# The 64-row parts of two products' low weights, in pairs of matmuls on the upper and lower rows of the array

## The chip, the cores and the metric

The kernel runs on one core of a Trainium2 chip. The metric is the device time of one execution in microseconds (us); the median of three runs of the kernel before is 1816.04 us (1814.41 to 1816.51). A core has five engines with a queue of instructions each: TensorE (PE in the profile; its weight loads are listed as PEld), VectorE (DVE), ScalarE (ACT), GpSimd (POOL) and SyncE (SP), which here only issues transfers. An engine works its queue in order. Engines wait for each other through semaphores.

## The reference

The input `x` has 8192 rows of 448 numbers. It is normalised row by row, and the result `xn` goes two ways:

```
xn = layernorm(x)                                   # 8192 x 448
s  = irfft( softshrink( mlp2( relu( mlp1( rfft(xn) )))))   # along the 8192 rows; 4 blocks of 112 channels
g  = silu( (gelu(xn @ w_gate) * (xn @ w_up)) @ w_down )    # 448 -> 1792 -> 448
out = x + s * g
```

`s` is the spectral part, `g` the feed-forward part, and the change lies in the feed-forward part's first two products, `xn @ w_up` and `xn @ w_gate`, which have a contraction of 448 = 3 x 128 + 64.

## The kernel before

Float32 numbers are held as two float16 numbers, high and low, and a product of two such numbers is three matmuls: high by high, high by low, low by high. The feed-forward products go by a scheme of seven products on halves of the operands (numbered 1 to 7 in the code, in the order 1, 5, 6, 2, 3, 7, 4), where sums and differences of the operands are made ahead. The rows of `x` are taken in 16 chunks of 512 rows, a chunk as two half chunks of 256, and the 1792 hidden columns in 14 tiles of 128. There are two passes over the chunks: the first with 8 of the tiles, whose weights stay in fast memory, the second with the other 6 (`PF`, line 30). The first two chunks of the first pass are done in a plain way. In all others the tiles are taken two at a time; such a pair is a *unit* (line 1026): four units for a chunk of the first pass, three for one of the second, 14 x 4 + 16 x 3 = 104 in all.

In a unit the seven products add up in three banks of the accumulator memory: X (ring `bx`, two banks), Y and Z (ring `by`, two banks). `a1` to `a7` are the steps that issue one product each, for both tiles of the unit:
- `a1` puts product 1 into X, ScalarE copies it out (`p1`); `a5` puts product 5 into Y, ScalarE copies it (`p5`); `a6` adds product 6 into X, ScalarE copies it (`v1`).
- `a2` puts product 2 into Z, and then VectorE adds Z to `p1` (`c11`, rows `u<-by,u` in the profile), ScalarE applies gelu to the sum.
- `a3` adds product 3 into Y, and VectorE adds Y to `v1` (`c12`, rows `v<-by,v`), then multiplies it with the gelu (rows `wt<-v,fc,u` in the second pass), which gives half of `h`.
- `a7` adds product 7 into X, and VectorE adds X and `p5` into `v2` (`c22`, rows `v<-bx,u`).
- `a4` adds product 4 into X. It waits until `c22` has read X. Then ScalarE applies gelu straight from X and VectorE multiplies it with `v2` (`c21`).

Products 1, 5, 6 and 7 are of two blocks of 128 rows: six matmuls for a tile, 12 for a unit. Products 2, 3 and 4 are of 192 rows, that is of one block of 128 rows and one of 64. The block of 128 takes three matmuls. In the block of 64 rows (`v + 1` and `xb + 1` in `product`, line 985) the high weights stand twice, in the upper and in the lower 64 rows, and the operand from `x` has its high part in one half of the rows and its low part in the other; so one matmul of 128 rows gives high by high and high by low. The fifth matmul of the five is low weights by the same operand. So products 2, 3 and 4 take 5 matmuls for a tile, 10 for a unit, each of 256 columns.

The order of a unit's steps is the list at the end of `unit` (line 1154); `a4` of a unit is issued ahead of the third step of the next one (`chunk`, line 1442). The last unit of a chunk has no next one. In the first pass, the down projection of the earlier tiles then stands between (`down`, line 1365). In the second pass `down2` (line 1251) begins with that `a4`; here, and only here, the list of before has `a7` ahead of `a3`.

All instructions are issued by a planner (`Pace`, line 49): tasks are generators, each with a due time; an instruction gets a cost by `Pace.cost` (line 168), and a task goes on when the planner's clock says that its input is there. It fixes the order in every engine's queue at build time, nothing more; on the chip the engines only follow it. `B` (class `Either`, line 204) gives an operation to VectorE or to GpSimd, whichever ends first by these costs. Beside the first pass the planner runs the first stage of the transform and the making of operands (`factors`, line 532, writes the sums of halves of `xn` that the products use to a scratch tensor, from which they are read transposed); beside the second pass the spectral stage (`group`, line 1702) and, after it, the last transform (`tiles3`, line 1814). Their matmuls stand between those of the units; they use the ring `bf`.

Every instruction is recorded by one helper, so all rows have line 199, and groups are told apart by the names of their tiles: `wt` are weights (of which two serve as buffers in the second pass), `xta` and `xtb` the transposed operands (`xtb` that of products 2, 3 and 4), `h` the hidden values, `dw` the weights down, `u,mt` the last transform.

Of the kernel before, what the change touches and what calls it, by code (L numbers as in the profile page):

```python
# [10 lines left out]
F16 = mybir.dt.float16  # L11
# [18 lines left out]
PF = ((0, 8), (8, 6))  # L30
PB = ((0, 5), (5, 8))
K1, K2 = 256, 192
# [16 lines left out]
class Pace:  # L49
# [118 lines left out]
    def cost(self, e, op, start, out, ins):  # L168

        n, sb, psum = self.wide(out, ins)  # L170
        extra = sum(n > 1 and i.free_size() == 1 for i in ins)
        if e == "PE":
            n = out.free_size()
            return max(0.049, n * 0.000423 + 0.001) * (4 if ins[0].dtype == F32 and op == "matmul" else 1)
        if e == "ACT":
            return (0.14 if psum else 0.18) + 0.00086 * n + 0.1 * extra
        if e == "POOL":
            t = 1.1 if n < 8 and op == "tensor_tensor_pow" else 0.2 + 0.0023 * n
        elif n < 32:
            return 0.17  # L180
        elif psum or sb < 2 and op != "tensor_scalar":
            return 0.14 + 0.00107 * (n + 60 * (extra > 0))
        else:
            t = (0.12 + 0.00112 * n if sb >= 2 else 0.15 + 0.0008 * n) + 0.06 * (extra > 0)
        other, ahead = ("POOL", 0.15) if e == "DVE" else ("DVE", 0.0)
        return t + max([b - start - ahead for a, b in self.port[other] if a <= start < b] + [0.0])
# [187 lines left out]
def afno_geglu_kernel(ctx, tc, x, gu, wd, mlp, b1, b2, c_m, c_mt, c_small, out):  # L374
    nc = tc.nc
    pace = Pace()
    V, S, G, T, Q = (Engine(pace, n, e) for n, e in (
        ("DVE", nc.vector), ("ACT", nc.scalar), ("POOL", nc.gpsimd), ("PE", nc.tensor), ("SP", nc.sync)))
    B = Either(pace, V, G, 0.0)
# [50 lines left out]
    wt = [cp.tile([128, 2, 16, 128], F16, name=f"wt{f}") for f in range(PF[0][1])]  # L430
# [26 lines left out]
    EV = {}  # L457

    def ev(*key):
        return EV.setdefault(key, Event())  # L460
# [71 lines left out]
    def factors(c, q, xs):  # L532

        xn = EV["x4", c][:, 2 * q:2 * q + 2, :]
        sf = yield from SF.get()
        sx = yield from SX.get()
        S.copy(sf[:, 0, K2:], xn[:, 1, K2:K1])
        B.tensor_add(sf[:, 0, 0:K2], xn[:, 1, 0:K2], xn[:, 1, K1:])
        B.tensor_sub(sf[:, 2, :], xn[:, 0, 0:K1], xn[:, 1, 0:K1])
        yield  # L540
        B.tensor_sub(sf[:, 1, :], sf[:, 0, :], xn[:, 0, 0:K1])
        yield
        B.tensor_sub(sf[:, 3, 0:K2], xn[:, 0, K1:], sf[:, 1, 0:K2])
        big = sx[:, 0:6 * K1].rearrange("p (k s c) -> p k s c", k=3, s=2)
        low = sx[:, 6 * K1:]
        S.copy(big[:, :, 0, :], sf[:, 0:3, :])
        yield
        S.copy(low[:, 0:K2], sf[:, 3, 0:K2])
        B.tensor_sub(big[:, :, 1, :], sf[:, 0:3, :], big[:, :, 0, :])
        yield  # L550
        B.tensor_sub(low[:, K2:K1], sf[:, 3, 128:K2], low[:, 128:K2])
        B.tensor_sub(low[:, K1:], sf[:, 3, 0:128], low[:, 0:128])
        SF.put(sf)
        yield
        rows = xts[c % NG][128 * q:128 * q + 128]
        Q.dma_start(rows[:, 2 * K1:2 * K1 + 4 * 480], sx)
        SX.put(sx)
        yield ev("lo", c, q)
        Q.dma_start(rows[:, 0:2 * K1].rearrange("p (s c) -> p s c", s=2), xs[:, 0, :, 0:K1])
        low = rows[:, 2 * K1 + 4 * 480:].rearrange("p (k c) -> p k c", k=2)  # L560
        Q.dma_start(low[:, :, 0:K2], xs[:, :, 0, K1:])
        Q.dma_start(low[:, :, K2:K1], xs[:, :, 1, D - 64:])
        Q.dma_start(low[:, :, K1:], xs[:, :, 1, K1:K1 + 128])
        yield
# [410 lines left out]
    PROD = {1: (0, 4), 5: (4, 8), 6: (8, 10), 7: (12, 12), 2: (3, 6), 4: (6, 14), 3: (0, 2)}  # L975
# [6 lines left out]
        yield  # L982
        done("xt", kind, first, i)

    def product(k, bank_, xT, f0, first, last):
        xb, v = PROD[k]
        for e in range(2):
            w = wt[f0 + e]
            if k in (1, 5, 6, 7):
                seq = [(s, v + j, xb + 2 * d + j) for j in range(2) for s, d in ((0, 0), (0, 1), (1, 0))]  # L990
            else:
                seq = [(0, v, xb), (0, v, xb + 2), (1, v, xb), (0, v + 1, xb + 1), (1, v + 1, xb + 1)]
            for n, (s, vv, xx) in enumerate(seq):
                T.matmul(bank_[:, 256 * e:256 * e + 256], w[:, s, vv, :], xT[:, xx, :],
                         start=first and e == 0 and n == 0, stop=last and e == 1 and n == len(seq) - 1,
                         skip_group_check=True)


    state = {"direct": NG}

# [5 lines left out]
    def gelu(p, f0, gl, src):  # L1006
        for cs, b in scaled(p, f0):
            S.activation(gl[:, cs], src[:, cs], AF.Gelu_apprx_tanh, scale=fc[:, 4, b:b + 1])
# [17 lines left out]
    def unit(p, i, f0, h, xa):  # L1026

        m = {}
# [9 lines left out]
        def a1():  # L1038
            for e in range(2):
                yield ev("comb", f0 + e) if p == 0 else ev("far", f0 + e)  # L1040
            m["X"] = yield from BX.get()
            product(1, m["X"], xa, f0, True, False)
            copy_of(U1, "p1", m["X"], pace.last)

        def a5():
            m["Y"] = yield from BY.get()
            product(5, m["Y"], xa, f0, True, False)
            copy_of(U5, "p5", m["Y"], pace.last)

        def a6():  # L1050
            yield m["ep1"]
            product(6, m["X"], xa, f0, False, False)
            copy_of(V1, "v1", m["X"], pace.last)

        def a2():
            m["Z"] = yield from BY.get()
            product(2, m["Z"], EV["xtb", p, i], f0, True, True)
            m["c11"] = pace.spawn(c11(), pace.last)

        def c11():  # L1060
            u = m["p1"]
            V.tensor_tensor(u, m["Z"], u, op=ALU.add)
            BY.put(m["Z"])
            yield
            gelu(p, f0, u, u)
            yield

        def a3():
            yield m["ep5"]
            product(3, m["Y"], EV["xtb", p, i], f0, False, True)  # L1070
            pace.spawn(c12(), pace.last)

        def c12():
            yield m["ev1"]
            v = m["v1"]
            V.tensor_tensor(v, m["Y"], v, op=ALU.add)
            BY.put(m["Y"])
            yield
            yield m["c11"]
            if p == 1:  # L1080
                g0 = m["g0"] = yield from G0.get()

                def back():
                    V1.put(v)
                    U1.put(m["p1"])

                yield from glu(p, f0, m["p1"], v, 0, h, back, g0)
                done("h", p, i, f0, 0)
                return
            yield from glu(p, f0, m["p1"], v, 0, h, lambda: V1.put(v))  # L1090
            U1.put(m["p1"])
            done("h", p, i, f0, 0)
# [33 lines left out]
        def sums(gl):  # L1126
# [24 lines left out]
            G0.put(g0)  # L1151
            pace.then(lambda: done("hs", i, f0, 0))

        return [a1, a5, a6, a2, a7, a3] if p == 1 and f0 == PF[1][1] - 2 else [a1, a5, a6, a2, a3, a7], a4

    def plain(c, f):

# [284 lines left out]
    def chunk(p, i):  # L1442
# [19 lines left out]
        for u in range(nf // 2):  # L1462
            six, last = unit(p, i, 2 * u, h, xa)
            for n, s in enumerate(six):
                if (u, n) == (0, 2) and "tail" in state:
                    yield from state.pop("tail")()
                if (u, n) == (0, 3):
                    yield ev("xt", "b", p, i)
                if n == 2 and prev:
                    yield from prev()  # L1470
                    if (p, i) == (0, NG - 1):
                        pace.spawn(far_pair(u - 1))
                    yield pe()
                yield from s()
                yield pe()
            prev = last
# [639 lines left out]
```

## Time and profile before

| | us |
|---|---|
| median of three runs | 1816.04 |
| span of the profiled execution, first to last instruction | 1811.1 |
| TensorE busy | 1769.5 (98%) |
| VectorE busy | 1395.7 (77%) |
| ScalarE busy | 1059.9 (59%) |
| GpSimd busy | 470.3 (26%) |
| granted TensorE clock, mean | 0.998 |

The page gives the span of the profiled execution and no other time of its own; the median of the runs is 4.9 us longer.

A row of a group reads: line, engine, operation, tile written <- tiles read, shapes, count, then after the bar the busy time in us, the mean time of one in ns, and the idle time of the engine just before them with what ended it. A matmul's shape 128*128 is rows and columns of the array, and then what streams through. A row of the timeline reads: start in us, length in us, engine, line, operation, shape and count; in brackets stands idle time before it and what ended it. Matmuls are pipelined: the length of a row holds the time until its last result is out, so a matmul's slot is read from the distance of two starts.

### The profile page before, as it was taken

What the parts mean: (1) busy time and instruction counts of PE and PEld (TensorE: products, weight loads), DVE (VectorE), ACT (ScalarE), POOL (GpSimd) and SP (SyncE); (2) the same over time, 40 slices, a digit from 0 to 9 for tenths busy, and PEclk for the clock granted to TensorE, in tenths of its full rate; (3) what the DMA queues carried; (4) which work ended last, traced back from release to release, by engine and by line L of the source; (5) the groups of instructions that cost most, each with busy time, mean ns of one, the idle gap of its engine ahead of it and who ended that gap; (6) DMA issues with size and microseconds to landing.
All of it is one profiled execution on the core that took longest, in us unless ns stands there. A gap on an engine that the chain in (4) does not pass through costs nothing. (4 is left out here: it accounts for less than half of the span.)

```text
span 1811.1 us, 39096 instructions
## 1 busy us (share of the span) xinstructions
PE 1769.5 (98%) x15709; PEld 1429.6 (79%) x15709; DVE 1395.7 (77%) x2497; ACT 1059.9 (59%) x2015; POOL 470.3 (26%) x550
## 2 busy tenths in 40 slices
PE   7999999999999999999999999999999999999997
PEld 3447777767687777787887999999999998888886
DVE  7867888777865656656766888889888887888876
ACT  5746555645555444556676777777777674333343
POOL 3333432432221122100110322233223222232331
PEclk9999999999999999999999999999999999999999
DMA  6554776468655433322335624444335438999971
GB/s 217 159 151 125 201 202 193 148 196 233 168 131 162 135 111 94 94 66 75 88 126 155 163 83 119 119 109 92 94 104 119 114 80 222 296 303 304 291 234 44
DMA packets 345733, 277.03 MB, mean 153 GB/s; under 512 B 231536, under 2 KB 316784, under 8 KB 345552
## 3 DMA queue, kind: packets, MB, share of 16 engines
q1 hardware_dynamic: 345264, 273.98, 53.5%
q8 instruction: 123, 2.02, 0.5%
q10 hardware_dynamic: 288, 0.56, 0.1%
q14 instruction: 58, 0.48, 0.1%
HBM read 123.31 MB, written 102.02 MB: 124 GB/s over the span
## 5 line engine op out<-in xcount | busy, mean ns | idle before, releaser
L199 PEld LDWEIGHTS <-wt 128*128 128x128 f16 x9350 | 909.7, 98 | 173.3 <-issue 17.8
L199 PE MATMUL bx<-xta,wt 128*128 128x256 f16 (+1 forms) x3843 | 473.6, 275 | 0.3 <-ACT v L199 0.2
L199 PEld LDWEIGHTS <-h 128*128 128x128 f16 x2688 | 257.1, 98 | 131.8 <-DVE h L199 4.5
L199 PE MATMUL bd<-dw,h 128*128 128x448 f16 (+1 forms) x1920 | 345.5, 329 | 3.4 <-DVE h L199 2.8
L199 PE MATMUL by<-xtb,wt 128*128 128x256 f16 x2080 | 251.2, 272 | 0.0
L199 PE MATMUL by<-xta,wt 128*128 128x256 f16 (+1 forms) x1347 | 177.0, 281 | 4.1 <-DVE xta L199 3.1
L199 POOL TENSOR_TENSOR wt<-wt 128x256 f32<-128x256 f32 x90 | 72.1, 801 | 304.4 <-DVE wt L199 288.0
L199 PE MATMUL bx<-xtb,wt 128*128 128x256 f16 x1040 | 130.5, 272 | 1.8 <-DVE v L199 0.9
L199 DVE TENSOR_TENSOR u<-by,u 128x512 f32<-128x512 f32 x104 | 71.5, 688 | 57.3 <-PE by L199 55.7
L199 ACT COPY u<-bx 128x512 f32<-128x512 f32 x104 | 60.9, 585 | 74.4 <-PE bx L199 73.3
L199 ACT ACTIVATE u<-u,fc 128x512 f32<-128x512 f32 (+1 forms) x118 | 77.6, 668 | 41.9 <-DVE u L199 41.9
L199 PE MATMUL bd<-dw,wt 128*128 128x224 f16 (+1 forms) x816 | 96.0, 264 | 4.7 <-DVE pt L199 4.5
L199 ACT COPY v<-bx 128x512 f32<-128x512 f32 x104 | 60.8, 585 | 63.9 <-PE bx L199 63.4
L199 ACT CAST h<-wt 128x512 f16<-128x512 f32 (+1 forms) x128 | 68.8, 538 | 47.3 <-DVE wt L199 37.4
L199 DVE SCALAR_TENSOR_TENSOR pt<-bd,fb,pt 128x448 f32<-128x448 f32 x96 | 63.5, 680 | 39.1 <-PE bd L199 38.9
L199 ACT COPY u<-by 128x512 f32<-128x512 f32 x104 | 61.0, 587 | 52.5 <-PE by L199 48.6
L199 ACT ACTIVATE th<-bd,fb 128x448 f32<-128x448 f32 x62 | 39.1, 632 | 83.5 <-PE bd L199 71.6
L199 PE MATMUL bf<-w2t,wn 112*128 112x112 f16 x1512 | 84.9, 213 | 0.0
L199 DVE SCALAR_TENSOR_TENSOR gl<-v,fc,gl 128x512 f32<-128x512 f32 (+1 forms) x70 | 47.8, 699 | 45.6 <-ACT gl L199 45.4
L199 PEld LDWEIGHTS <-wn 112*128 112x128 f16 x1512 | 80.6, 98 | 2.4
L199 DVE TENSOR_TENSOR v<-by,v 128x512 f32<-128x512 f32 x104 | 71.0, 683 | 6.4 <-PE by L199 5.8
L199 PEld LDWEIGHTS <-w1t 112*112 112x112 f16 x612 | 68.6, 130 | 7.9 <-issue 3.3
(218 smaller groups left out, 3037.7 us busy)
## 6 DMA issues: line engine op xcount, KB each, us to landing
xts<-sx SPq DMA_DIRECT2D x32, 480.0 KB, 3.1
x<-in_x SPq DMA_DIRECT2D x17, 896.0 KB, 6.4
t<-ysb SPq DMA_DIRECT2D x64, 224.0 KB, 3.3
prt<-th SPq DMA_DIRECT2D x64, 224.0 KB, 2.2
pt<-prt SPq DMA_DIRECT2D x64, 224.0 KB, 3.9
u<-t SPq DMA_DIRECT2D x32, 448.0 KB, 5.7
x<-in_x SPq DMA_DIRECT2D x32, 448.0 KB, 6.2
y<-t SPq DMA_DIRECT2D x30, 448.0 KB, 4.0
```

Of the source, the lines that this page charges most:

```text
L199: return self.pace.issue(self.name, kind, out, ins, lambda: fn(out, *args, **kw))
```

## The change

For products 2 and 3 the fifth matmul (low weights of the 64-row block) is left out of `product` and done by a new function `half`, with 64 rows of the array instead of 128: product 2 on the upper half of the rows and into Z, product 3 on the lower half and into Y. `a3` issues them after product 3, for each tile first product 2's and then product 3's, so that two neighbours use different halves of the array's rows and different banks. Product 2's bank is complete only then, so `c11` is started behind them. The operand of product 3 must have its high part in the lower half of the rows for this, so `factors` writes the two parts the other way round, with one more copy. The exception in the order of the last unit of a chunk of the second pass is dropped: all units have `a3` before `a7`. The planner's cost of a matmul with 64 rows becomes half of the formula's value plus a constant (first part of the diff).

```diff
@@ Pace.cost
             n = out.free_size()
+            if op == "matmul" and ins[0].shape[0] == 64 and ins[0].dtype == F16:
+                return 0.5 * (n * 0.000423 + 0.001) + 0.03
             return max(0.049, n * 0.000423 + 0.001) * (4 if ins[0].dtype == F32 and op == "matmul" else 1)
@@ factors
-        S.copy(low[:, 0:K2], sf[:, 3, 0:K2])
+        S.copy(low[:, 0:128], sf[:, 3, 0:128])
+        S.copy(low[:, K2:K1], sf[:, 3, 128:K2])
         B.tensor_sub(big[:, :, 1, :], sf[:, 0:3, :], big[:, :, 0, :])
         yield
-        B.tensor_sub(low[:, K2:K1], sf[:, 3, 128:K2], low[:, 128:K2])
+        B.tensor_sub(low[:, 128:K2], sf[:, 3, 128:K2], low[:, K2:K1])
@@ product
-    def product(k, bank_, xT, f0, first, last):
+    def product(k, bank_, xT, f0, first, last, whole=True):
+
         xb, v = PROD[k]
+        last = last and whole
...
                 seq = [(0, v, xb), (0, v, xb + 2), (1, v, xb), (0, v + 1, xb + 1), (1, v + 1, xb + 1)]
+                seq = seq[0:5 if whole else 4]
...
+    def half(k, bank_, xT, f0, e):
+
+        at = 64 * (k == 3)
+        xb, v = PROD[k]
+        T.matmul(bank_[:, 256 * e:256 * e + 256], wt[f0 + e][at:at + 64, 1, v + 1, :], xT[at:at + 64, xb + 1, :],
+                 start=False, stop=e == 1, skip_group_check=True)
@@ unit
-            product(2, m["Z"], EV["xtb", p, i], f0, True, True)
-            m["c11"] = pace.spawn(c11(), pace.last)
+            product(2, m["Z"], EV["xtb", p, i], f0, True, True, False)
...
-            product(3, m["Y"], EV["xtb", p, i], f0, False, True)
+            product(3, m["Y"], EV["xtb", p, i], f0, False, True, False)
+            for e in range(2):
+                half(2, m["Z"], EV["xtb", p, i], f0, e)
+                half(3, m["Y"], EV["xtb", p, i], f0, e)
+            m["c11"] = pace.spawn(c11(), pace.last)
             pace.spawn(c12(), pace.last)
...
-        return [a1, a5, a6, a2, a7, a3] if p == 1 and f0 == PF[1][1] - 2 else [a1, a5, a6, a2, a3, a7], a4
+        return [a1, a5, a6, a2, a3, a7], a4
```

## The prediction

> **What bounds the kernel now.** I read the page first: engine shares and the clock row.
>
> ```profile
> span 1811.1 us, 39096 instructions
> ...
> PE 1769.5 (98%) x15709; PEld 1429.6 (79%) x15709; DVE 1395.7 (77%) x2497; ACT 1059.9 (59%) x2015; POOL 470.3 (26%) x550
> ...
> PEclk9999999999999999999999999999999999999999
> ```
>
> TensorE is busy for 98% of the span at a full clock, so what matters is the length of its own instruction stream: a slot that leaves it is a gain, and a gap put into it is a loss that no other engine can give back. The second view is busy time by stretch, cut where the passes of the feed-forward part meet: its first pass, its second pass beside the spectral stage, its second pass beside the last transform.
>
> ```profile
> 160.00:884.00 724.00, 719.64 (x5784) 548.66 (x5782) 518.33 (x961) 405.36 (x747) 181.53 (x244) 1.00 0.50 140
> 884.00:1410.00 526.00, 523.27 (x5531) 465.81 (x5530) 434.96 (x757) 379.96 (x757) 130.71 (x129) 1.00 0.46 118
> 1410.00:1800.00 390.00, 381.04 (x3638) 340.88 (x3636) 317.79 (x517) 182.78 (x341) 111.17 (x113) 1.00 0.73 216
> ```
>
> The columns after the length are TensorE, its weight loads, VectorE, ScalarE and GpSimd. TensorE is over 97% busy in all three; VectorE is at 72%, 83% and 81%, and so has room on average, but not at every moment. The third view is the group of matmuls that the change cuts into, and the fourth is the order in time around a unit that is the last of its chunk in the second pass (TensorE and VectorE rows).
>
> ```profile
> L199 PE MATMUL by<-xtb,wt 128*128 128x256 f16 x2080 | 251.2, 272 | 0.0
> ```
>
> ```profile
> 1554.95 1.26 PE L199 MATMUL by<-xtb,wt 128*128 128x256 f16 x10
> ...
> 1556.04 1.47 PE L199 MATMUL bx<-xta,wt 128*128 128x256 f16 x12
> ...
> 1557.13 0.68 DVE L199 TENSOR_TENSOR u<-by,u 128x512 f32<-128x512 f32 x1
> 1557.35 1.25 PE L199 MATMUL by<-xtb,wt 128*128 128x256 f16 x10
> 1557.73 0.68 DVE L199 TENSOR_TENSOR v<-bx,u 128x512 f32<-128x512 f32 x1
> ...
> 1558.44 0.73 PE L199 MATMUL bf<-u,mt 128*128 128x448 f16 x3
> ...
> 1559.01 1.26 PE L199 MATMUL bx<-xtb,wt 128*128 128x256 f16 x10
> ...
> 1560.12 0.74 DVE L199 SCALAR_TENSOR_TENSOR wt<-v,fc,u 128x512 f32<-128x512 f32 x1
> ```
>
> 2080 matmuls are 104 units of 20 (products 2 and 3). Starts give a matmul's slot: 1557.35 to 1558.44 is 1.09 us for ten, so 0.109 us for 256 columns; 1558.44 to 1559.01 gives 0.19 us for 448. The order here is product 2, 7, 3, then three matmuls of the last transform, then product 4. Product 4 adds into the bank that VectorE must first read (v<-bx at 1557.73, done at 1558.41). Product 3 and the other matmuls are what hides that read: product 4 starts at 1559.01 and waits for nothing.
>
> **The pairs.** Each unit loses four matmuls of 128 rows and gets four of 64 rows, in two pairs, in one block after product 3. Removed: 4 x 0.109 = 0.436 us. The built program marks the 832 instructions of these blocks (416 matmuls, 416 weight loads) as using 64 of the array's rows. The trace shows what it costs to leave the 128x128 form and return, on the few matmuls that do so:
>
> ```profile
> 258.45 1.11 PE L199 MATMUL bd<-dw,h 128*128 128x448 f16 x5
> 259.49 0.38 PE L199 MATMUL bf<-identf,fx 128*2 128x128 f32 x2
> 259.81 1.31 PE L199 MATMUL bd<-dw,h 128*128 128x448 f16 x6
> 261.05 0.38 PE L199 MATMUL bf<-identf,mxr 2*128 2x2 f32 x2
> ```
>
> ```profile
> 50.55 0.95 PE L199 MATMUL bd<-ident,xs 128*128 128x128 f16 x8
> 51.43 0.82 PE L199 MATMUL by<-xta,wt 128*128 128x512 f16 x3
> ```
>
> ```profile
> 1053.36 0.83 PE L199 MATMUL bf<-sm,y 128*112 128x128 f16 x12
> 1054.03 1.25 PE L199 MATMUL by<-xtb,wt 128*128 128x256 f16 x10
> ```
>
> Five slots of 0.19 from 258.45 end at 259.40, and the matmul on 2 columns starts at 259.49: 0.09 lost. Six slots from 259.81 end at 260.95, and the one on 2 rows starts at 261.05: 0.10 lost, and this one changes rows as the edit does. The eight transposes at 50.55 hold two that write 64 rows only (the row shows the commonest shape). At the slot of a 128-column matmul, (1054.03 - 1053.36)/12 = 0.056, they would take 0.45; they take 0.88, so each visit to the other form and back costs 0.43/2 = 0.215 us. I count one visit for a block, since its four matmuls are of one form. [...]
>
> What four 64-row matmuls cost once inside is not in the trace. Lower bound: each pair fully side by side, 2 x 0.109 = 0.218. Upper bound: one after the other, 0.436. Between them lies one weight load that isn't hidden. Its pace comes from the shortest matmuls with a load each:
>
> ```profile
> 1049.15 1.34 PE L199 MATMUL bf<-w2t,wn 112*128 112x112 f16 x24
> 1050.33 1.31 PE L199 MATMUL bd<-dw,h 128*128 128x224 f16 x12
> ```
>
> 1.18/24 = 0.049 us. I take 0.218 + 0.049 = 0.267: the upper half starts one load after the lower, and then both run on. The block is 0.215 + 0.267 = 0.482 against 0.436: a loss of 0.046 per unit, 104 x 0.046 = **+4.8 us**. Ends: 0.215 + 0.218 is 0.433, no change (-0.3 us); 0.215 + 0.436 is +0.215 per unit, +22.4 us. [...]
>
> **Product 2's add moves behind product 3.** VectorE's add of product 2 (c11) started after product 2 and now comes behind the block, next to product 3's add (c12). In units that are not the last of a chunk this costs nothing: the next user of a `by` bank is the next unit's product 5, which stands 24 matmuls (2.6 us) after the block, and the add needs 0.9. ScalarE's gelu and the product for `h` follow 1 us later than before; their reader is the down projection of later units.
>
> **The order in the second pass's last unit.** The edit also drops the exception that put product 7 ahead of product 3 there. In the built order of the changed program the block is followed by product 7 and then, in the last seven of the 16 chunks, at once by product 4; the cover in the rows at 1557.35 and 1558.44 is gone. VectorE's queue there holds c11, c12, up to three other operations, and only then the read of product 7's bank. Prices:
>
> ```profile
> 1542.33 0.73 PE L199 MATMUL bf<-u,mt 128*128 128x448 f16 x3
> 1542.90 1.25 PE L199 MATMUL bx<-xtb,wt 128*128 128x256 f16 x10
> ```
>
> ```profile
> 1543.10 0.68 DVE L199 SCALAR_TENSOR_TENSOR g<-bf,ms,g 128x448 f32<-128x448 f32 x1 [1.53 <-PE bf L199]
> ...
> 1545.76 0.42 DVE L199 TENSOR_TENSOR wt<-wt 128x256 f32<-128x256 f32 x1
> 1546.10 0.68 DVE L199 SCALAR_TENSOR_TENSOR g<-bf,ms,g 128x448 f32<-128x448 f32 x1
> ...
> 1548.03 0.68 DVE L199 TENSOR_TENSOR u<-by,u 128x512 f32<-128x512 f32 x1
> 1548.63 0.68 DVE L199 TENSOR_TENSOR v<-by,v 128x512 f32<-128x512 f32 x1
> ```
>
> ```profile
> 1570.96 1.28 DVE L199 SCALAR_TENSOR_TENSOR pt<-bd,fb,pt 128x448 f32<-128x448 f32 x2 [0.17 <-PE bd L199]
> 1571.70 2.46 PE L199 MATMUL bd<-dw,wt 128*128 128x224 f16 x24 [0.20 <-DVE pt L199]
> ```
>
> TensorE's stream passes on at 1542.90 and an idle VectorE starts at 1543.10: 0.20. Back to back, 512 columns take 0.60 (1548.03 to 1548.63), 256 take 0.34 (1545.76 to 1546.10). The first add of the pair at 1570.96 ends 0.68 later, at 1571.64, and TensorE starts at 1571.70: 0.06. From the end of the block, product 4 may start at 0.20 + 2 x 0.60 + X + 0.68 + 0.06 = 2.14 + X, X being what else is in VectorE's queue; TensorE has 12 x 0.109 = 1.31 of product 7 and what stands beside it. Nor may it start before product 7's end + 0.94. From the built order:
> - last seven chunks: two with X = 0.34 + 0.60 + 0.75 and 0.57 more cover, 1.95 each; two with X = 0.34, 1.17 each; two with X = 0.60, 1.43 each; one with nothing, 0.94. Sum 10.0.
> - first nine chunks, where the spectral stage's matmuls stand between: 0.76, 0, 0.61, 1.79, 0.55, 0.73, 0.37, 0.33, 0.73. Sum 5.9.
>
> So **+15.9 us**, with 0 in place of it today. Lower end: no queue, only the 0.94 less the cover after product 7: 6.6 + 4.1 = 10.7. Upper end: VectorE is late by what it was late at 1557.13 (1.09 after the stream's end instead of 0.20), 16 x 0.89 more: 30.1. A gain is excluded: nothing lets product 4 start earlier. Behind it everything on TensorE's queue waits.
>
> **The rest** I cost at nothing. Factors: 32 more ScalarE copies, hidden in ScalarE's idle time (405 of 724 us busy). The planner's other choices move 33 operations from GpSimd to VectorE, among them 38 of the group below (others go back), and 38 x 0.45 = 17 us of VectorE is inside its slack of 91 + 72 us in the last two stretches. SP issues the same transfers as before.
>
> ```profile
> L199 DVE TENSOR_TENSOR wt<-wt 128x256 f32<-128x256 f32 x102 | 45.6, 447 | 4.5 <-POOL wt L199 3.0
> ```
>
> **The sum.** 1811.1 + 4.8 + 15.9 = 1831.8 us of span. The median of the runs is 4.9 above this execution's span, and I take that as what lies around it: **1837 us**, against 1816.04. A change of 0.2% (3.6 us) is about what a measurement of this kernel can tell from none.
>
> **The rivals.**
> - *The halves do not run side by side.* Nothing in the trace shows two matmuls at once; only the bank of each half (Z and Y) speaks for it. Then 22.4 + 15.9: 1854 us.
> - *The change of form is free between half and full rows* (the other side). Then each unit gains 0.436 - 0.267 to 0.436 - 0.218, that is 17.6 to 22.7 us, less 15.9: 1809 to 1814, at best 7 us faster. It decides below 0.03 us per visit with full overlap; the 0.10 us at 261.05, for a form of few rows, speaks against it. [...]
> - *The wait before product 4 does not come*, since VectorE is early or the loss is taken back in waits like the 0.20 at 1571.70. Then +4.8, or nothing with full overlap: 1816 to 1821. The built order speaks against it.
>
> **How the numbers follow.** Forecast (pairs overlap, form costs, product 4 waits) 0.70, by its own bounds 1811.1 + 4.9 - 0.3 + 10.7 = 1826 to 1811.1 + 4.9 + 4.8 + 30.1 = 1851; no overlap 0.12; free change of form 0.08; no wait 0.10. The range from 1820 to 1856 leaves out the free form and most of the last case, under 2 in 10. Faster 0.07 (from the free form), same 0.08 (the rest of it and most of the last case), slower 0.85.
>
> **What would show it.** In the changed profile: each unit has a group of four matmuls on 64 rows, 0.09 to 0.10 us after the slot before it, about 0.48 us to the next full matmul; in a wrong case 0.22 to 0.27 or 0.65. TensorE waits for VectorE `v` 14 to 16 times, 0.4 to 2 us each, in the second pass only, and the first pass is longer by 56 x 0.046 = 2.6 us and no more. The prediction is wrong if the block is under 0.40 us, or if those waits sum to under 8 us.

## The result

The changed kernel takes 1835.4 us (median of four runs, 1834.62 to 1838.02), the kernel before 1815.2 us on the same chip. The ratio is 1.0115, 95% interval 1.0101 to 1.013: slower by 20 us. The prediction was 1837, from 1820 to 1856. The total came out, but of its two terms one was too high and the other too low.

The page of the changed kernel, in the lines shown of before:

```profile
span 1833.6 us, 39171 instructions
...
PE 1773.5 (97%) x15709; PEld 1394.0 (76%) x15709; DVE 1394.4 (76%) x2530; ACT 1058.9 (58%) x2047; POOL 439.5 (24%) x517
...
PEclk9999999999999999999999999999999999999999
```

The span is 22.5 us longer, TensorE has the same number of matmuls, and is busy 97% instead of 98%: it stood still longer. Its waits add up to 51.2 us, where they were 32.0. The mean granted clock is 0.996 against 0.998. The view of waits (who waited for whom, us in total, times, longest) has one new row at its head; the second fence is the same row of before.

```profile
PE bx L201 <- DVE v L201: 21.7, 17, 2.8
PE bd L201 <- DVE fx L201: 8.0, 1, 8.0
PE bd L201 <- DVE pt L201: 5.1, 15, 1.2
```

```profile
PE bx L199 <- DVE v L199: 0.9, 3, 0.5
```

Product 4 waits 21.7 us for VectorE's read of its bank, 20.8 more than before. That is most of the loss. Fifteen of the 17 waits, 20.8 us, lie in the last units of the second pass's chunks; none of the three of before does. The timeline of one such place (last unit of a chunk, TensorE, VectorE and GpSimd):

```profile
1522.76 2.23 PE L201 MATMUL by<-xtb,wt 128*128 128x256 f16 x20
...
1524.83 2.32 POOL L201 TENSOR_TENSOR wt<-wt,wt 128x512 f16<-128x512 f32 x2 [6.25 <-ACT wt L201]
1524.92 0.74 PE L201 MATMUL bf<-u,mt 128*128 128x448 f16 x3
1525.02 0.69 DVE L201 TENSOR_TENSOR u<-by,u 128x512 f32<-128x512 f32 x1
...
1525.50 1.47 PE L201 MATMUL bx<-xta,wt 128*128 128x256 f16 x12
1525.63 0.68 DVE L201 TENSOR_TENSOR v<-by,v 128x512 f32<-128x512 f32 x1
...
1526.23 1.20 DVE L201 TENSOR_TENSOR h<-wt,h 128x256 f16<-128x256 f32 x1
1527.36 0.67 DVE L201 SCALAR_TENSOR_TENSOR g<-bf,ms,g 128x448 f32<-128x448 f32 x1
1527.95 0.73 DVE L201 SCALAR_TENSOR_TENSOR wt<-v,fc,u 128x512 f32<-128x512 f32 x1
...
1528.61 0.68 DVE L201 TENSOR_TENSOR v<-bx,u 128x512 f32<-128x512 f32 x1
...
1529.34 1.63 PE L201 MATMUL bx<-xtb,wt 128*128 128x256 f16 x10 [2.37 <-DVE v L201]
```

Product 7 has streamed by 1526.81 (12 slots of 0.109 from 1525.50). VectorE then still has a subtraction, the last transform's product and the product for `h` ahead of the read `v<-bx,u`, and TensorE starts product 4 at 1529.34, 2.5 us later. (The view of waits gives 2.37: it counts from the end of the last matmul's row, some 0.16 us behind the end of its slot.)

Such a wait can cost more than its length, here 1.7 us more. TensorE's rows behind this one, and the granted clock (the third number from the right) from 1520 to 1530 and in the 3.4 us behind it:

```profile
1529.34 1.63 PE L201 MATMUL bx<-xtb,wt 128*128 128x256 f16 x10 [2.37 <-DVE v L201]
1530.77 1.32 PE L201 MATMUL bf<-u,mt 128*128 128x448 f16 x3
1531.89 2.09 PE L201 MATMUL bd<-dw,h 128*128 128x224 f16 x12
1533.82 1.31 PE L201 MATMUL by<-dw,h 128*128 128x224 f16 x12
1534.96 0.26 PE L201 MATMUL bd<-dw,wt 128*128 128x224 f16 x1
```

```profile
1520.00:1530.00 10.00, 7.63 (x69) 6.12 (x68) 8.16 (x14) 5.26 (x9) 3.84 (x3) 1.00 0.78 299
1530.00:1533.40 3.40, 3.40 (x18) 2.17 (x16) 1.50 (x4) 0.69 (x1) 0.00 (x0) 0.51 0.13 24
```

The first three rows take 4.48 us from start to start. At full clock ten matmuls on 256 columns take 1.09, three on 448 take 0.58 (1524.92 to 1525.50) and twelve on 224 take 1.14 (1533.82 to 1534.96), 2.81 in all: 1.7 us are lost. The same happens behind the longest wait (2.78 us, up to 1577.65), and behind no other wait of the second pass in this run, the next longest being 2.11 us. So 3.4 us of the loss are clock. This is not a rule for waits of a certain length: in experiment 2 below, one of 3.14 us has no such stretch behind it, and in experiment 1 one of 1.96 us has. The clock row of the page, in slices of 46 us, does not show these stretches.

The pairs themselves, by shape (groups of the changed kernel; busy us and mean ns after the bar):

```profile
L201 PE MATMUL by<-xtb,wt 128*128 128x256 f16 x1664 | 202.4, 273 | 0.0
...
L201 PE MATMUL by<-xtb,wt 64*128 64x256 f16 x416 | 40.8, 274 | 0.0
```

And in the timeline of the changed kernel a unit's products 2 and 3 with their block, up to product 7 at the second row:

```profile
1666.94 2.23 PE L201 MATMUL by<-xtb,wt 128*128 128x256 f16 x20
...
1669.11 1.48 PE L201 MATMUL bx<-xta,wt 128*128 128x256 f16 x12
```

From start to start this is 2.17 us. In the kernel before the same two products took 2.18:

```profile
1536.22 2.35 PE L199 MATMUL by<-xtb,wt 128*128 128x256 f16 x20
1538.40 2.78 PE L199 MATMUL bx<-xta,wt 128*128 128x256 f16 x24
```

Between the single starts of all 104 blocks the trace of the changed kernel has, at the median, 0.096 us more than a slot on the way in, 0.003 to 0.004 from a matmul of the pair to its partner, 0.116 to the second pair, 0.202 from the last start to the next full matmul, and 0.010 more in that one's own slot. With the slot before taken off this is 0.420 + 0.010 = 0.430 against 0.436: the gain of the pairs and the price of the form cancel, at 0.6 us for 104 units.

### The profile page after: what moved, and what is told of

The parts are those of the page before. It is cut to its first block, busy times and chain, and to the rows that moved or that the text cites. A ratio compares the mean times of both kernels' runs of the same rounds, so it can differ in the third digit from the quotient of the medians.

```text
span 1833.6 us, 39171 instructions
## 1 busy us (share of the span) xinstructions
PE 1773.5 (97%) x15709; PEld 1394.0 (76%) x15709; DVE 1394.4 (76%) x2530; ACT 1058.9 (58%) x2047; POOL 439.5 (24%) x517
## 3 DMA queue, kind: packets, MB, share of 16 engines
HBM read 123.31 MB, written 102.02 MB: 123 GB/s over the span
## 5 line engine op out<-in xcount | busy, mean ns | idle before, releaser
L201 PEld LDWEIGHTS <-wt 128*128 128x128 f16 (+1 forms) x9350 | 875.6, 98 | 226.2 <-issue 77.1
L201 PE MATMUL by<-xtb,wt 128*128 128x256 f16 (+1 forms) x2080 | 236.2, 273 | 0.0
L201 PE MATMUL bx<-xtb,wt 128*128 128x256 f16 x1040 | 131.7, 274 | 22.0 <-DVE v L201 21.7
L201 POOL TENSOR_TENSOR zs<-t,zs 112x256 f16<-112x256 f32 (+1 forms) x40 | 31.2, 780 | 273.9 <-ACT zs L201 269.1
L201 POOL TENSOR_TENSOR wt<-wt,wt 128x512 f16<-128x512 f32 x50 | 60.4, 1217 | 110.3 <-ACT wt L201 83.5
L201 DVE TENSOR_TENSOR h<-wt,h 128x512 f16<-128x512 f32 (+1 forms) x87 | 71.2, 818 | 16.0 <-ACT h L201 15.7
L201 ACT ACTIVATE th<-pt 128x448 f32<-128x448 f32 x64 | 36.9, 576 | 66.3 <-DVE pt L201 66.1
```

Of the source, the lines that this page charges most:

```text
L201: return self.pace.issue(self.name, kind, out, ins, lambda: fn(out, *args, **kw))
```

## The experiments

The theory from these rows: the loss is the wait before product 4, from the dropped order and the moved add; the pairs are neutral. The rival: the pairs or the change of form cost part of it.

**1. The order put back.** The one line of the order in the last unit of the second pass is that of before; pairs, block and moved add stay.

```diff
-        return [a1, a5, a6, a2, a3, a7], a4
+        return [a1, a5, a6, a2, a7, a3] if p == 1 and f0 == PF[1][1] - 2 else [a1, a5, a6, a2, a3, a7], a4
```

> The changed kernel with the order of before in the last unit of the second pass's chunks (product 7 ahead of product 3). If the loss is the wait before product 4 alone: the waits on `v` fall from 21.7 us to under 4, and the time to 1813 to 1816 us, since the block measured 0.430 us against 0.436. If the pairs cost something that the trace's block does not show: it stays above 1820.

Measured: 1819.8 us, 1.0037 (1.0024 to 1.0049) of before, 15.6 us below the changed kernel.

```profile
PE bx L201 <- DVE v L201: 2.0, 3, 0.9
```

The waits are gone, as the theory has it. The time is 4 us above what it expected, and that needed a cause of its own.

**2. The order alone.** The kernel before, with the exception dropped and nothing else.

```diff
-        return [a1, a5, a6, a2, a7, a3] if p == 1 and f0 == PF[1][1] - 2 else [a1, a5, a6, a2, a3, a7], a4
+        return [a1, a5, a6, a2, a3, a7], a4
```

> The kernel before with only that order dropped: all products whole, product 2's add where it was. VectorE's queue then lacks product 2's add at that place. If the order alone makes the loss: plus 20 us, 1835. If half of it is product 2's add, put behind the block and ahead of the read in VectorE's queue: each wait is about 0.6 us shorter, 16 x 0.6 = 10 us, so plus 8 to 12 us, 1823 to 1827.

Measured: 1851.9 us, 1.0212 (1.0198 to 1.0226). Neither value: the order alone costs 37 us, more than the whole change. The waits on `v` account for 29 of it (30.1 us against 0.9), and behind five of them the granted clock is 0.5 for 3.41 us, 1.7 lost each time, some 8 more. The waits and one place of the timeline:

```profile
PE bx L199 <- DVE v L199: 30.1, 18, 3.1
```

```profile
1532.59 1.47 PE L199 MATMUL bx<-xta,wt 128*128 128x256 f16 x12
...
1533.66 1.12 DVE L199 SCALAR_TENSOR_TENSOR wt<-v,fc,u 128x512 f32<-128x512 f32 x1
1534.33 1.46 POOL L199 TENSOR_TENSOR wt<-wt,wt 128x512 f16<-128x512 f32 x1
1534.70 1.63 DVE L199 TENSOR_TENSOR wt<-wt,wt 128x512 f16<-128x512 f32 x1
...
1536.26 0.68 DVE L199 TENSOR_TENSOR v<-bx,u 128x512 f32<-128x512 f32 x1
...
1536.99 1.79 PE L199 MATMUL bx<-xtb,wt 128*128 128x256 f16 x8 [2.93 <-DVE v L199]
```

With product 2's add early, the product for `h` is ready early too, and the planner puts it (1533.66) and a subtraction (1534.70) ahead of the read. They take 1.12 and 1.63 us; GpSimd works beside both (1533.56 to 1535.79). My expectation took one operation out of VectorE's queue and did not ask what would move up. In this run the product for `h` stands ahead of the read in 11 of the 16 last units, in the changed kernel in 3. So there the moved add makes the dropped order cheaper, not dearer, as far as two different plans can be compared.

**3. Two visits for a unit.** On experiment 1: each tile's pair stands right behind that tile's part of product 3.

```diff
-            product(3, m["Y"], EV["xtb", p, i], f0, False, True, False)
             for e in range(2):
+                product(3, m["Y"], EV["xtb", p, i], f0, False, True, False, e)
                 half(2, m["Z"], EV["xtb", p, i], f0, e)
                 half(3, m["Y"], EV["xtb", p, i], f0, e)
```

> As the first run, with the pair of each tile right behind that tile's part of product 3, so two visits to the 64-row form for a unit instead of one. If a visit costs 0.20 to 0.21 us, as the trace of the changed kernel has it (0.205 - 0.109 in, 0.202 - 0.109 + 0.010 out): plus 104 x 0.206 = 21 us on the first run. If the price comes only once for a unit or is hidden: within 5 us of it.

Measured: 1837.7 us, 17.9 above experiment 1.

```profile
1647.16 2.45 PE L201 MATMUL by<-xtb,wt 128*128 128x256 f16 x20
1649.54 1.48 PE L201 MATMUL bx<-xta,wt 128*128 128x256 f16 x12
```

2.38 instead of 2.17 us for the 20 matmuls: a visit costs 0.21 us, as predicted from the transposes (0.215). The other engines' queues are in the order of experiment 1. 104 x 0.21 is 22 us; the total shows 18. TensorE's waits are 2.8 us shorter here (33.0 in all against 35.8), which is most of the difference.

**4. Both on the same half of the rows.** On experiment 1: `at = 0` for both products, and the operand laid out as in the kernel before.

```diff
-        at = 64 * (k == 3)
+        at = 0
```

> As the first run, with both products' 64-row matmuls on the upper half of the rows (the operand of product 3 is laid out as before for it). If the pairs gain by running side by side: each pair then takes 0.109 us more, plus 208 x 0.109 = 23 us on the first run. If matmuls on the same half overlap as well: no change.

Measured: 1836.8 us, 17.0 above experiment 1.

```profile
1661.89 2.45 PE L201 MATMUL by<-xtb,wt 128*128 128x256 f16 x20
1664.27 1.48 PE L201 MATMUL bx<-xta,wt 128*128 128x256 f16 x12
```

Again 2.38: without different rows each unit takes 0.21 us more, that is two slots of 0.109. So in these runs the pairs do run side by side, and what they gain, 0.21 us for a unit, is what a visit costs. The total shows 17 and not the 22 us of 104 x 0.21: TensorE's waits are 3.9 us shorter here (31.9 in all), and the plan is not quite that of experiment 1.

**5. The block left out.** On experiment 1, without the four 64-row matmuls: the low weights of the 64-row blocks of products 2 and 3 are not applied.

```diff
             product(3, m["Y"], EV["xtb", p, i], f0, False, True, False)
-            for e in range(2):
-                half(2, m["Z"], EV["xtb", p, i], f0, e)
-                half(3, m["Y"], EV["xtb", p, i], f0, e)
             m["c11"] = pace.spawn(c11(), pace.last)
```

> As the first run, with the four 64-row matmuls of each unit left out (the low weights of the 64-row blocks of products 2 and 3 are not applied). If the block costs what its starts show, 0.430 us: 104 x 0.430 = 45 us less than the first run, 1775 us. If the pairs have a cost elsewhere on TensorE: more than 48 us less. If waits behind the block take its place: clearly less than 45.

Measured: 1794.7 us, 25 below experiment 1 and not 45. The last product 4 of the second pass, in experiment 1 and then here:

```profile
1791.46 1.26 PE L201 MATMUL bx<-xtb,wt 128*128 128x256 f16 x10
```

```profile
1747.60 1.25 PE L201 MATMUL bx<-xtb,wt 128*128 128x256 f16 x10
...
1766.07 1.30 PE L201 MATMUL bf<-u,mt 128*128 128x448 f16 x6
1772.34 4.66 PE L201 MATMUL bf<-u,mt 128*128 128x448 f16 x12 [4.97 <-DMA mt<-c_mt]
```

Up to there it is 43.9 us ahead, 0.42 for a unit. That is near the 0.430 of the starts, but two things that are not the block are in it. This plan begins the last transform a chunk later, and 51 of its matmuls, which experiment 1 has behind it by then, are still to come (8.6 us at their slots of 0.19 and 0.096, an estimate); and TensorE's waits up to there are 6.2 us longer (39.6 against 33.4). With both taken out it is 41.5 us, 0.40 for a unit, so the block's price is borne out to some 7%. Of the 43.9 us some 20 come back at the end (the profiled spans differ by 23.7): the 51 matmuls, 5.9 us of waits for their loads, and a granted clock of 0.50 from 1770.4 to 1777.0.

**6 and 7. Whole matmuls or pairs, under one plan.** Experiment 6 is experiment 1 with the four matmuls on all 128 rows. Experiment 7 is experiment 1 with the planner's cost of a 64-row matmul set back to that of any other. The built orders of the two are the same on every engine, instruction by instruction; only the rows differ.

```diff
# 6
-        T.matmul(bank_[:, 256 * e:256 * e + 256], wt[f0 + e][at:at + 64, 1, v + 1, :], xT[at:at + 64, xb + 1, :],
+        T.matmul(bank_[:, 256 * e:256 * e + 256], wt[f0 + e][:, 1, v + 1, :], xT[:, xb + 1, :],
# 7
-            if op == "matmul" and ins[0].shape[0] == 64 and ins[0].dtype == F16:
-                return 0.5 * (n * 0.000423 + 0.001) + 0.03
```

> As the first run (product 7 ahead of product 3 in the last units), with the four matmuls of the block on all 128 rows, so no change of form and no pairs; product 2's add still stands behind the block. If pairs and whole matmuls cost the same (0.430 against 0.436 us): 1818 to 1823 us, as the first run, and what the first run is above the kernel before comes from the moved add. If the pairs cost 5 us: 1815.

> As the first run, with the planner's cost of a 64-row matmul set back to that of any other (0.109 us, so 0.436 for the block, which takes 0.430 on the chip, where the changed formula says 0.339). If the 5 us that the first run is above the kernel before come from orders planned on a block that is too short: 1813 to 1816 us. If they come from the moved add: no change, 1818 to 1821.

Measured: 1828.6 us with whole matmuls (1826.3 to 1829.7), 1829.2 us with pairs (1828.0 to 1831.1). This is the cleanest answer on the pairs: no difference. But both are 9 us slower than experiment 1, which differs from 7 by the planner's cost alone. The expected direction was the opposite.

**8. The dropped order with whole matmuls.** The changed kernel with the block on all 128 rows (and so planned at the full cost).

```diff
-        T.matmul(bank_[:, 256 * e:256 * e + 256], wt[f0 + e][at:at + 64, 1, v + 1, :], xT[at:at + 64, xb + 1, :],
+        T.matmul(bank_[:, 256 * e:256 * e + 256], wt[f0 + e][:, 1, v + 1, :], xT[:, xb + 1, :],
```

> As the changed kernel (product 7 behind product 3 in all units), with the four matmuls of the block on all 128 rows: the moved add and the dropped order without pairs. If these two make the whole loss: 1833 to 1839 us, as the changed kernel. If the 64-row form has a part in it: under 1830.

Measured: 1851.4 us, outside both values, and 22.8 above experiment 6, which is the same with the order put back. Without any 64-row matmul the loss of the order is there; it is larger than the 15.6 us between the changed kernel and experiment 1, again under another plan.

**9, 10 and 11. How much is the plan?** 9 is the kernel before with only the planner's cost of the fifth matmuls of products 2 and 3 set to 0.085 us. 10 is experiment 1 with 0.061 in place of 0.085. 11 is experiment 1 with the block behind product 2 in all units but the last ones of the second pass, which puts product 2's add back to its old place there.

```diff
# 9
+            if op == "matmul" and self.low:
+                return 0.5 * (n * 0.000423 + 0.001) + 0.03
...
+                pace.low = k in (2, 3) and n == 4
# 10
-                return 0.5 * (n * 0.000423 + 0.001) + 0.03
+                return 0.5 * (n * 0.000423 + 0.001) + 0.006
# 11, in a2
+            if not end:
+                yield m["ep5"]
+                pairs(False)
+                m["c11"] = pace.spawn(c11(), pace.last)
```

> The kernel before, with nothing changed but the planner's cost of the fifth matmuls of products 2 and 3 (0.085 us instead of 0.109). If the lower cost makes better orders as such: 1806 to 1811 us, since the run with the full cost was 9 us slower than the one with the lower. If it is only luck of one plan against another: anywhere within 1810 to 1825.

> As the first run (pairs, order of before), with the planner's cost of a 64-row matmul at 0.061 us, so the step from 0.109 to 0.085 made once more. If a shorter planned block gives better orders: 1811 to 1816 us. If the steps are luck of the plan: no trend, 1815 to 1830.

> As the first run, with the block right behind product 2 instead of product 3 in all units but the last ones of the second pass, so that product 2's add starts where it did before. If the moved add costs the 5 us that the first run is above the kernel before: 1812 to 1816 us. If they are luck of the plan: 1815 to 1825.

Measured: 1824.5, 1826.5 and 1826.2 us, with 1815.1 for before. Experiment 9 computes what the kernel before computes, by another plan, and that costs 9 us. The plan is more than the order in the queues: VectorE has three operations more and GpSimd three fewer (2500 and 547 instead of 2497 and 550), and the last transform begins a chunk later, so that one chunk more goes through the chip's main memory (123.31 MB read before, 124.23 here; 10 has the same). 10 is slower than experiment 1 where a trend would make it faster, and 11 does not get the 5 us back. Three pairs of kernels differ by the planner's cost alone, and in time by 9 us (before and 9), 9 us (1 and 7) and 6 to 7 us (1 and 10). So the 5 us of experiment 1 lie within what a new plan does, and no run here can put them down to the moved add or to the pairs. In the traces most of such a difference is TensorE's waits: 32.0 us in all before, 35.8 in 1, 43.7 and 44.8 in 6 and 7, 40.1, 40.1 and 40.5 in 9, 10 and 11. What makes one plan wait longer than another was not followed up. No version was found that beats the kernel before with the work whole.

## Why the prediction was right

**The pairs: mechanism right, size off.** Predicted +4.8 us, with -0.3 as the lower end; the starts say -0.6, just outside. Right were the loss on the way in (0.09 to 0.10, measured 0.096), one visit for a block, and 0.215 for a visit (0.21 in experiment 3). The step that failed is "one weight load that isn't hidden", 0.049: partners start 0.003 to 0.004 us apart. That a block is one visit I assumed, and no row of before shows it; in the changed kernel the second pair starts 0.116 us after the first one's second matmul, 0.007 more than a slot, so the 0.096 is paid once, and in experiment 3 a second visit costs 0.21. The rivals "no overlap" and "free change of form" are both refuted, by experiments 4 and 3.

**The dropped order: right place, right reason, too small.** Predicted +15.9 us of waits for `v` in the second pass's last units, measured +20.8, and some 23 if counted from the end of the slot as the prediction does. Experiment 1 takes them away with one line, experiment 8 shows the loss without pairs. For the place shown above the prediction had 1.95 (X = 0.34 + 0.60 + 0.75); TensorE lost 2.5. The mis-sized term is X: the subtraction, priced at 0.34 from a row where GpSimd was idle, took 1.13 from its start to the next one (1526.23 to 1527.36), and here GpSimd was at work. The same subtraction stands ahead of the read in eight of the 16 last units, and takes 0.99 to 1.53 us from its start to the next one in each. In the four of the last seven chunks, where the prediction lists its terms, that is 3.3 us more than 4 x 0.34. These seven measured 11.7 for 10.0, since two places without that operation came out shorter than forecast (1.16 for 1.43); the first nine measured 9.1 for 5.9.

**"The rest costs nothing": wrong as a step.** The planner's other choices were counted as free because VectorE has slack. Experiments 7 and 9 show that another plan by itself can cost around 9 us. In the changed kernel this term is small: the last two products 4 of the first pass start 2.4 and 3.1 us later than before. It could as well have been 10, and the sum had no term for it. Nor had it one for the clock, which it took as full: 3.4 us. All of TensorE's waits together grow by 19.2 us; with 3.4 for the clock and -0.6 for the pairs that is 22.0 of the 22.5 us of span.

**Luck.** That 1837 came within 2 us is luck: 4.8 us that did not come stand against waits that were too small and a clock that was not counted. So is the first pass: 2.6 us were forecast for it, for the pairs, and it is 2 to 3 us longer, but there the pairs save 0.3.

**The chances.** Slower at 0.85 was the case, by 1.15%, where 0.2% was given as the least that can be told; the wait that was said to come did come, with the count foreseen in the last units (14 to 16, 15 measured; the other two waits, 0.2 and 0.7 us, are elsewhere). It was to be 0.4 to 2 us each; 0.2 to 2.8 was measured.

## What to carry to other kernels

Price a change of the array's form as a visit: here 0.2 us in and out, so two pairs of 256-column matmuls only pay for the visit, and by these numbers a block would have to hold more pairs than that to gain (no run here has such a block). When an order in a full queue is changed, write down what every engine has queued between the event and the reader, since here the cover that was dropped was worth more than the matmuls that were saved. Read the granted clock behind a long wait too; here two of them cost 1.7 us each on top of their length. Where a planner fixes the order, run the old kernel under a disturbed plan first; differences below that scatter cannot be put down to a single edit.

## What was not expected

Some of VectorE's operations took much longer beside GpSimd (1.205 us against 0.415 at the median for one shape), others did not (0.691 with it and without). The tiles of `h` in the changed kernel (VectorE; min, median and max in ns):

```profile
L201 DVE TENSOR_TENSOR h<-wt,h x87: 408/692/1753, 1009.3 to 1816.3; 128x512 f16<-128x512 f32 x55, 128x256 f16<-128x256 f32 x32
```

Of the 32 subtractions on 256 columns, the seven that start with GpSimd idle, or within 15 ns of its end, take 0.415 us at the median, the 25 that start while it works 1.205. All of these 25 end 0.28 to 0.29 us after the end of a GpSimd instruction. The add `u<-by,u`, which reads one operand from the accumulator memory, takes 0.691 in both cases. It also fell the other way round: in the kernel before, seven such subtractions take 0.41 us though GpSimd's row began 0.41 us ahead of them, and there it is GpSimd's row that is long, 1.83 to 1.85 us, where the shortest of the same shape take 1.16. No run here shows what makes the one or the other row long. That VectorE's long rows are what makes the waits longer than forecast is a reading of the rows; no kernel was run that keeps GpSimd still there.
